# Between two MLPs: the second sequence's rows, sums and operands placed anew around the first quads

## The chip, the cores and the metric

The kernel runs on one NeuronCore of a Trainium2 chip. The metric is the device time of one execution in microseconds; lower is better.

## What is computed

Three layers follow each other: a block-wise linear attention with decay, an MLP with a squared relu, and a gated MLP with a norm in front. Cut to what matters here:

```python
x = attn_out.transpose(0, 2, 1, 3).reshape(B * S, H * D)    # 2 sequences x 768 tokens, 512 features

h = x @ w_in                                  # first MLP, 512 -> 2048
x = (s * relu(h) ** 2 + b) @ w_out            # 2048 -> 512

rms = np.sqrt(np.mean(x * x, axis=-1, keepdims=True) + 1e-06)
xn = x / rms * rms_g                          # the norm between the MLPs
g = xn @ w_gate                               # second MLP, 512 -> 1536
val = xn @ w_val
return (silu(g) * val) @ w_out
```

All of it is float32. A float32 product is made of three matmuls in a reduced format (`PASSES`): each operand is split into a high part (a copy that rounds) and a low part (what is left), and high x high, high x low and low x high are summed in PSUM.

## The kernel before

Tokens lie along the free dimension and features along the 128 partitions. A sequence is 768 tokens; a product over one takes 512 and 256 columns.

**First MLP.** `for blk in range(B)` goes over the two sequences, and within a block `it` goes over 16 tiles of hidden features. TensorE makes the hidden tile of `it` (`h` and `hb`, one bank each) and adds the products of the tile before to `y` (four banks, 512 tokens each) and `z` (two banks, two pieces of 256 tokens in each). ScalarE and VectorE make relu, square, scale and the split of the tile (`relu2`, `gate_hi1`, `gate_lo1`; the split goes to the tile `g`). Beside that, prepared work is drawn from a list `todo`: `work(n)` runs the next n tasks at a fixed place of an iteration.

**Between the MLPs.** When a block's sums are done, `take` and `take2` bring them from PSUM to the rows `xq[blk]`, times the norm's gain `g_col`; `square` writes their squares to `xtmp[blk]`. `norm_total` adds the squares of the four feature tiles on VectorE; `norm_rstd` sums over partitions on TensorE (`nps`), takes the power -1/2 on GpSimd and lays it on a diagonal (`affine_select`); `norm_apply` broadcasts it by a matmul with ones (`rb`) and scales the rows on VectorE. `x_tasks` then makes the seven operands of the second MLP from the rows: four differences t1 to t4 (`sub`) and seven splits (`x_split`: ScalarE writes the high part, VectorE the low part). For the first sequence all this lies inside the second block. For the second it lies in the first quads.

**Second MLP.** Gate, value, the two halves of the features and the two halves of a sequence's tokens form 2 x 2 blocks, multiplied with seven block products in place of eight. A *quad* (`quad(i)`) is one tile of 128 hidden features on one sequence: seven products of six matmuls of 384 columns, in four PSUM banks, quads 0, 2, 4 in banks 0 to 3 and quads 1, 3, 5 in banks 4 to 7. Products b0, b1, b2, b3 come first; ScalarE copies b0 (`q1`), and VectorE's adds `add(u2, b1, q1)`, `add(u3, b2, u2)`, `add(u3, b3, u3)` carry the sums on. Then three products are added on top in b0, b2 and b3 (called b0', b2', b3' below); b2' may start when the add from b2 is done, b3' when the add from b3 is. ScalarE makes the two silus, and `a_mult` multiplies silu and value, one quad later. Quads 0 to 3 take the first sequence, quad 4 is the first on the second; from quad 8 on both alternate.

**What sets the order.** The schedule is manual: every engine runs its instructions as the code emits them, in order. A quad yields after parts of its products; at each `(quad, part)` the table `plan` says which tasks of the second sequence are emitted, and `work()` draws from `todo` (weight tasks). Weight set f of the second MLP is made by `w_tasks(f)`, six tasks with scalings, four GpSimd sums and splits; sets 0 to 3 in the second block, but for the last three tasks of set 3 (`w_last`), which stand in `plan`. Before, parts 0, 1 and 2 of a quad end after the add from b1, after the add from b3, and at its end.

**Rooms.** `xq0` and `xq1` hold the rows, `g` the first MLP's split tile. Squares of the second sequence go to `g` (`xtmp.append(rows(m_g))`), operands of the second sequence lie in `xs`, `xq0` and `wm`, and later products of `a_mult` in `g`.

VectorE's take and ScalarE's square of one PSUM bank are ordered one behind the other by a wait, in the order of the code.

Of the kernel before, what the change touches and what calls it, by code (L numbers as in the profile page):

```python
# [22 lines left out]
def attention_moe_moe2_kernel(  # L23
# [40 lines left out]
    NG1 = 4  # L64
# [469 lines left out]
    xtmp = [xq[1]]  # L534
# [11 lines left out]
    def x_tasks(s, other):  # L546
        b11, b12, b21, b22 = (x_block(s, k, h) for k in range(2) for h in range(2))
        t1, t2, t3, t4 = (x_sum(s, i) for i in range(4))

        def sub(engine, to, a, b):  # L550
            engine.tensor_tensor(to, a, b, op=ALU.subtract)

        def first():
            sub(nc.vector, t1, b12, b11)
            sub(nc.vector, t2, b22, t1)

        def second():
            sub(other, t3, b22, b12)
            sub(other, t4, b21, t2)
            x_split(s, B11, b11)  # L560

        rest = ((T2, t2), (T3, t3), (T1, t1), (B21, b21), (T4, t4), (B22, b22))
        return [first, second] + [lambda op=op, src=src: x_split(s, op, src) for op, src in rest]
# [4 lines left out]
    def norm_total(s):  # L568
        x = xtmp[s]
        nc.vector.tensor_tensor(x[:, 0:2], x[:, 0:2], x[:, 2:4], op=ALU.add)  # L570
        nc.vector.tensor_tensor(x[:, 0], x[:, 0], x[:, 1], op=ALU.add)

# [19 lines left out]
    def norm_apply(s, cols, ps):  # L592
        nc.tensor.matmul(ps, ones, xtmp[s][:, 1, cols], start=True, stop=True)
        width = cols.stop - cols.start
# [18 lines left out]
    for blk in range(B):  # L613
# [4 lines left out]
        for it in range(NF1 + 1):  # L618
# [39 lines left out]
            work(blk)  # L658
# [11 lines left out]
            work(2 * blk)  # L670
            if blk == 0 and it == NF1 - 1:
                split_x(xs1, xq[1])
            if blk == 1:
                if it == 0:
                    norm_total(0)
                if it == 2:
                    norm_rstd(0, other)
                if it in (3, 4, 5):
                    norm_apply(0, slice((it - 3) * BX, (it - 2) * BX), other)
                if it == 5:  # L680
                    todo += x_tasks(0, nc.vector)
                    load_w(0, 0)
                    load_w(0, 1)
                if it == 8:
                    words = piece(early, "u1", 8, F32)
                    tasks = [w_tasks(f) for f in range(NG1)]
                    todo += sum(tasks, [])[:-3]
                    w_last = tasks[-1][-3:]

        if blk == 1:  # L690
            m_g = piece(early, "g", 12, F32)
            xtmp.append(rows(m_g))
# [20 lines left out]
        for d in (0, 2):  # L713
            square(NK + d // 2)
            take2(d)
            take2(d + 1)
# [4 lines left out]
    m_x2, m_wm2 = piece(early, "xq0", 12), piece(early, "wm", 6)  # L721
# [272 lines left out]
```

## Time and profile before

| | |
|---|---|
| median of 3 runs | 614.87 us (613.70 to 615.73) |
| profiled execution | 612.44 us, of which the span on the core is 610.6 us |
| TensorE matmul busy | 597.2 us, 98% of the span |
| TensorE weight loads | 540.3 us, 88% |
| VectorE, ScalarE, GpSimd busy | 368.8 us (60%), 299.1 us (49%), 72.5 us (12%) |
| chain that ended last | TensorE 90%, VectorE 5%, ScalarE 2% |

The profile gives one execution, in microseconds from the span's start. PE is TensorE, DVE VectorE, ACT ScalarE, POOL GpSimd. A row of a timeline is one instruction or several of one kind that follow each other; in square brackets stands how long the engine was idle before it and what released it. Rows of a timeline can overlap by some 0.1 us, since an engine starts an instruction before the last is quite done. The first block ends near 184 us, the second near 322 us, the quads run from there to about 507 us, and the output product ends the kernel.

### The profile page before, as it was taken

To read this page: it belongs to the slowest core of one execution; us is meant where nothing else is said; L and a number is where in the kernel's file an instruction comes from. 1 tells how busy PE (TensorE), PEld (TensorE's weight loads), DVE (VectorE), ACT (ScalarE), POOL (GpSimd) and SP (SyncE) were. 2 spreads that over 40 slices of the span, in tenths; PEclk is the share of its full clock that TensorE was granted. 3 is DMA by queue.
4 is the path that set the end of the run, shared out by engine and by line. 5 is a ranking of instruction groups with operands and counts; after the bars stand their busy time and mean duration, and the time that the engine had idled before them with its cause. 6 is when DMAs were issued, how large, how long until landed. Compare 5 with 4: busy or idle time off the path is not lost.

```text
span 610.6 us, 9226 instructions
## 1 busy us (share of the span) xinstructions
PE 597.2 (98%) x3654; PEld 540.3 (88%) x3654; DVE 368.8 (60%) x610; ACT 299.1 (49%) x549; POOL 72.5 (12%) x80
## 2 busy tenths in 40 slices
PE   8999999999999999999998799999999999999997
PEld 7888888888888888888887799999999998888886
DVE  6786776666745135444445976777777777875200
ACT  5685665565556224555554233444444445764200
POOL 3550000000000100011101500222222200000000
PEclk8999999999999999999999989999999999999999
DMA  8992533333100000022220001222122122220300
GB/s 321 368 347 96 181 116 127 130 112 138 69 1 1 0 2 1 0 70 70 69 69 2 0 2 39 90 79 70 69 70 70 69 70 70 104 104 0 139 34 35
DMA packets 17281, 51.97 MB, mean 85 GB/s; under 512 B 2390, under 2 KB 2390, under 8 KB 17238
## 3 DMA queue, kind: packets, MB, share of 16 engines
q1 hardware_dynamic: 17232, 51.39, 23.6%
q8 instruction: 28, 0.46, 0.3%
q14 instruction: 15, 0.12, 0.1%
q10 hardware_dynamic: 6, 0.00, 0.0%
HBM read 48.24 MB, written 3.15 MB: 84 GB/s over the span
## 4 chain that ended last, share of the span: by engine, by line
PE 90%; DVE 5%; ACT 2%; issue 1%; DMA 1%; SPq 0%; DVEq 0%; ACTq 0%
PE q L744 25%; PE out L886 16%; PE h L228 14%; PE y L631 14%; PE hb L228 7%; PE z L641 7%; PE sc L328 2%; PE o L370 2%; PE o L379 2%; PE st L396 1%; DMA k<-in_kT_dram 1%; DVE xs_None L150 1%; DVE r_None L755 1%; DVE xq_None L598 1%; DVE xq_None L702 1%
## 5 line engine op out<-in xcount | busy, mean ns | idle before, releaser
L744 PE MATMUL q<-u_None,u_None 128*128 128x384 f32 x504 | 91.9, 340 | 5.0 <-DVE st_None L755 3.6
L228 PE MATMUL h<-xs_None,u_None 128*128 128x512 f32 x384 | 94.1, 394 | 0.5 <-ACT r_None L241 0.5
L744 PEld LDWEIGHTS q<-u_None,u_None 128*128 128x128 f32 x504 | 88.9, 191 | 6.1 <-DVE st_None L755 4.2
L631 PE MATMUL y<-g_None,u_None 128*128 128x512 f32 x384 | 93.2, 391 | 0.0
L228 PEld LDWEIGHTS h<-xs_None,u_None 128*128 128x128 f32 x384 | 70.2, 188 | 14.3 <-ACT r_None L241 0.7
L631 PEld LDWEIGHTS y<-g_None,u_None 128*128 128x128 f32 x384 | 70.1, 188 | 13.3
L247 DVE TENSOR_SCALAR r_None<-r_None,params 128x768 f32<-128x768 f32 x32 | 21.8, 682 | 87.4 <-ACT r_None L243 87.4
L744 PE MATMUL q<-xs_None,u_None 128*128 128x384 f32 x288 | 55.2, 334 | 0.0
L641 PEld LDWEIGHTS z<-g_None,u_None 128*128 128x128 f32 x384 | 50.3, 191 | 2.5
L228 PEld LDWEIGHTS hb<-xs_None,u_None 128*128 128x128 f32 x384 | 50.3, 191 | 2.5
L641 PE MATMUL z<-g_None,u_None 128*128 128x256 f32 x384 | 51.0, 282 | 0.0
L228 PE MATMUL hb<-xs_None,u_None 128*128 128x256 f32 x384 | 51.0, 282 | 0.0
L241 ACT ACTIVATE r_None<-h 128x512 f32<-128x512 f32 x32 | 19.1, 598 | 64.1 <-PE h L228 63.0
L744 PEld LDWEIGHTS q<-xs_None,u_None 128*128 128x128 f32 x288 | 50.4, 188 | 0.0
L147 ACT ACTIVATE u_None<-u_None 128x768 fp32r<-128x768 f32 (+3 forms) x39 | 31.6, 822 | 32.7 <-DVE u_None L144 28.2
L253 DVE TENSOR_TENSOR g_None<-r_None,g_None 128x768 fp32r<-128x768 f32 x32 | 30.7, 958 | 24.6 <-ACT g_None L249 24.6
L150 DVE TENSOR_TENSOR u_None<-u_None,u_None 128x512 fp32r<-128x512 f32 (+2 forms) x51 | 37.6, 769 | 3.6 <-ACT u_None L147 3.5
L791 ACT ACTIVATE st_None<-r_None 128x384 f32<-128x384 f32 x24 | 12.6, 525 | 52.6 <-DVE r_None L755 52.6
L755 DVE TENSOR_TENSOR st_None<-q,r_None 128x384 f32<-128x384 f32 x48 | 26.5, 552 | 19.1 <-PE q L744 19.0
L512 POOL TENSOR_TENSOR u_None<-u_None 128x256 f32<-128x256 f32 x12 | 14.9, 1240 | 177.1 <-DVE u_None L144 177.1
L147 ACT ACTIVATE u_None<-wm_None 128x512 fp32r<-128x512 f32 x32 | 20.0, 625 | 27.9 <-DVE wm_None L144 27.9
L886 PE MATMUL out<-u_None,xs_None 128*128 128x512 f32 x144 | 32.8, 389 | 0.0
(138 smaller groups left out, 905.4 us busy)
## 6 DMA issues: line engine op xcount, KB each, us to landing
st_None<-in_w_dram SPq DMA_DIRECT2D x68, 512.0 KB, 3.3
kv<-in_kv_dram SPq DMA_DIRECT2D x12, 512.0 KB, 6.0
q<-in_qT_dram SPq DMA_DIRECT2D x12, 256.0 KB, 5.8
k<-in_kT_dram SPq DMA_DIRECT2D x12, 256.0 KB, 5.8
out_dram<-st_None SPq DMA_DIRECT2D x8, 256.0 KB, 2.5
out_dram<-u_None SPq DMA_DIRECT2D x4, 256.0 KB, 3.9
row<-in_lam_dram ACTq DMA_DIRECT2D x1, 0.0 KB
row<-in_s_dram ACTq DMA_DIRECT2D x1, 0.0 KB
```

The lines of the kernel that those rows point to most:

```text
L147: nc.scalar.activation(to, src, AF.Copy)
L150: nc.vector.tensor_tensor(to, src, hi.bitcast(F32), op=ALU.subtract)
L228: nc.tensor.matmul(ps, wt[:, wi, kk * P : (kk + 1) * P], xs[:, xi, kk, cols], start=n == 0, stop=n == 3 * NK - 1)
L241: nc.scalar.activation(r[:, 0:BT], ps[0], AF.Relu)
L247: nc.vector.tensor_scalar(r, r, s_col, b_col, op0=ALU.mult, op1=ALU.add)
L253: nc.vector.tensor_tensor(g2[:, 1, :], r, g2[:, 0, :].bitcast(F32), op=ALU.subtract)
L512: nc.gpsimd.tensor_tensor(s1, a21, a22, op=ALU.add)
L631: nc.tensor.matmul(acc[d], wt[:, wi, d * P : (d + 1) * P], gs[f][:, gi, 0:BT], start=f == 0 and pi == 0, stop=f == NF1 - 1 and pi == 2,)
L641: nc.tensor.matmul(acc2[d // 2][:, d % 2 * BX : (d % 2 + 1) * BX], wt[:, wi, d * P : (d + 1) * P], gs[f][:, gi, BT:BW], start=f == 0 and p ...
L744: nc.tensor.matmul(ps, w_set(f)[:, wi, wop * KC + kt * P : wop * KC + (kt + 1) * P], x_ops[s][xop][:, xi, kt, :], start=n == 0 and not mor ...
L755: nc.vector.tensor_tensor(to, ps, more, op=ALU.add)
L886: nc.tensor.matmul(ps, rows_[:, ai], w_out[f][:, wi, :], start=first and pi == 0, stop=last and pi == 2)
```

## The change

- The second sequence's squares go to `xq0` instead of `g`. Its operands four and five lie in `g` instead of `xq0`, and what lay in `g` later (a room of `a_mult`, three output weights) changes places with it likewise.
- `take2`, the 256-token takes, run on VectorE instead of ScalarE, in both blocks. In the second block, the second square of z and all four `take2` are emitted in quad 0 instead of ahead of it.
- A quad yields five times instead of three: after the copy of b0, after the add from b1, after the add from b2, after the add from b3, and at its end. `work()` runs at the three places where it ran.
- `norm_total` is two steps with the third add of quad 0 between them, and the sums over partitions follow the first product of quad 1 instead of all of quad 0. The broadcasts go to banks 2 and 3, and the two halves of the scaling are emitted at two places.
- `x_tasks` is eleven steps of one instruction or one split each, all differences on VectorE. For the second sequence two of the differences were on GpSimd. They stand at eleven places of quads 2 to 4, where eight tasks stood in quads 1 to 4.
- `a_mult` of quads 1, 2 and 3 runs on GpSimd instead of VectorE.
- In the second block, `work` draws by a table: the eleven tasks of the first sequence in iterations 6 and 7, all 24 weight tasks in iterations 8 to 15. Before, it drew three an iteration and left the last three weight tasks to the quads.

```diff
-    xtmp = [xq[1]]
+    xtmp = [xq[1], xq[0]]
...
-    def x_tasks(s, other):
+    def x_tasks(s):
+
         b11, b12, b21, b22 = (x_block(s, k, h) for k in range(2) for h in range(2))
         t1, t2, t3, t4 = (x_sum(s, i) for i in range(4))
...
+        return [
+            sub(t1, b12, b11),
+            sub(t2, b22, t1),
+            split(B11, b11),
+            split(T2, t2),
+            sub(t3, b22, b12),
+            split(T3, t3),
+            split(T1, t1),
+            split(B21, b21),
+            sub(t4, b21, t2),
+            split(T4, t4),
+            split(B22, b22),
+        ]
...
-            work(blk)
+            if blk:
+                work()
...
-            work(2 * blk)
+            if blk:
+                work({6: 4, 7: 5, 9: 1, 10: 3, 11: 2, 12: 3, 13: 3, 14: 2, 15: 2}.get(it, 0))
...
-            nc.scalar.activation(xq[blk][:, d, BT:BW], ps, AF.Copy, scale=g_col[:, d : d + 1])
+            nc.vector.tensor_scalar(xq[blk][:, d, BT:BW], ps, g_col[:, d : d + 1], None, op0=ALU.mult)
...
-        for d in (0, 2):
-            square(NK + d // 2)
-            take2(d)
-            take2(d + 1)
+        square(NK)
+        if blk == 0:
+            square(NK + 1)
+            for d in range(NK):
+                take2(d)
...
-            nc.vector.tensor_tensor(a_at[order[q]], v_both, silu, op=ALU.mult)
+            (nc.gpsimd if 1 <= q < NG1 else nc.vector).tensor_tensor(a_at[order[q]], v_both, silu, op=ALU.mult)
...
-        (0, 1): [lambda: norm_total(1)],
-        (0, 2): [lambda: start_second(0), w_last[0]],
-        (1, 0): [w_last[1]],
-        (1, 1): [lambda: start_second(1)],
-        (1, 2): [xt[0]],
-        (2, 0): [w_last[2], xt[1]],
-        (2, 1): [xt[2]],
-        (2, 2): [xt[3]],
-        (3, 0): [xt[4]],
-        (3, 1): [xt[5]],
-        (3, 2): [xt[6]],
-        (4, 0): [xt[7]],
-        (23, 0): [lambda: split_first(0)],
+        (0, 0): [lambda: square(NK + 1), lambda: take2(0), lambda: take2(1)],
+        (0, 2): [lambda: next(total)],
+        (0, 3): [lambda: next(total)],
+        (0, 4): [lambda: take2(2), lambda: take2(3)],
+        (1, 0): [lambda: norm_rstd(1, bank(1, "nps1"))],
+        (1, 3): [spread],
+        (1, 4): [lambda: scale[1]()],
+        (2, 0): xt[0:1],
+        (2, 1): xt[1:2],
+        (2, 3): xt[2:3],
+        (2, 4): xt[3:4],
+        (3, 0): xt[4:5],
+        (3, 1): xt[5:6],
+        (3, 2): xt[6:7],
+        (3, 4): xt[7:8],
+        (4, 0): xt[8:9],
+        (4, 1): xt[9:10],
+        (4, 2): xt[10:11],
+        (23, 1): [lambda: split_first(0)],
```

**ScalarE, from the end of the second block to quad 0's copy.** `y` and `z` are the block's sums, `q_0` is bank b0 of quad 0; the brackets name what a row waits for. Before:

```order
L696 ACTIVATE g_None<-y_1_1903 128x512 [waits DVE_49,PE_49]
L696 ACTIVATE g_None<-y_0_1902 128x512 [waits DVE_49]
L696 ACTIVATE g_None<-y_3_1905 128x512
L696 ACTIVATE g_None<-y_2_1904 128x512 [waits DVE_49]
L699 ACTIVATE g_None<-z_0_1906 128x2x256
L706 ACTIVATE xq_5_None<-z_0_1906,g_col 128x256 x2
L699 ACTIVATE g_None<-z_1_1907 128x2x256
L706 ACTIVATE xq_5_None<-z_1_1907,g_col 128x256 x2
L771 ACTIVATE st_20_None<-q_0_2916 128x384 [waits PE_49]
```

After:

```order
L704 ACTIVATE xq_4_None<-y_1_1903 128x512 [waits PE_49]
L704 ACTIVATE xq_4_None<-y_0_1902 128x512 [waits DVE_49]
L704 ACTIVATE xq_4_None<-y_3_1905 128x512 [waits PE_49]
L704 ACTIVATE xq_4_None<-y_2_1904 128x512 [waits DVE_49]
L707 ACTIVATE xq_4_None<-z_0_1906 128x2x256 [waits PE_49]
L780 ACTIVATE st_18_None<-q_0_2919 128x384 [waits PE_49]
L707 ACTIVATE xq_4_None<-z_1_1907 128x2x256
```

The four takes (L706) have left the engine, the squares go to another tile, and the copy of b0 has moved up by five instructions.

**VectorE, quad 3.** L755, then L764, are a quad's adds from PSUM (`q_1` to `q_3` are its banks b1 to b3), L763 is `a_mult`, L150 the low part of a split, L551, then L552, a difference. Before, from the add from b1 to that from b3':

```order
L755 TENSOR_TENSOR r_None<-q_1_3124,st_20_None 128x384
L150 TENSOR_TENSOR xs_None<-g_None,xs_None 128x768
L755 TENSOR_TENSOR st_20_None<-q_2_3125,r_None 128x384
L755 TENSOR_TENSOR st_20_None<-q_3_3126,st_20_None 128x384
L150 TENSOR_TENSOR xs_None<-xq_5_None,xs_None 128x768
L755 TENSOR_TENSOR st_20_None<-q_2_3125,r_None 128x384
L755 TENSOR_TENSOR r_None<-q_3_3126,r_None 128x384
```

After:

```order
L150 TENSOR_TENSOR g_None<-xq_4_None,g_None 128x768
L552 TENSOR_TENSOR xq_4_None<-xq_5_None 128x768
L764 TENSOR_TENSOR r_None<-q_1_3118,st_18_None 128x384
L150 TENSOR_TENSOR g_None<-xq_4_None,g_None 128x768
L764 TENSOR_TENSOR st_18_None<-q_2_3119,r_None 128x384
L150 TENSOR_TENSOR xs_None<-xq_4_None,xs_None 128x768
L764 TENSOR_TENSOR st_18_None<-q_3_3120,st_18_None 128x384
L764 TENSOR_TENSOR st_18_None<-q_2_3119,r_None 128x384
L764 TENSOR_TENSOR r_None<-q_3_3120,r_None 128x384
```

Each add from b1, b2 and b3 now has one piece of the second sequence ahead of it, and `a_mult` is no longer among the rows.

**GpSimd, quads 0 to 4.** L580, then L588, is the power, L582, then L590, the diagonal, L512 to L515 are sums of a weight set. Before:

```order
L580 TENSOR_TENSOR rstd_2981<-ms_2979,neg_half 128x6
L582 AFFINE_SELECT g_None<-rstd_2981 128x768
L512 TENSOR_TENSOR u_16_None<-u_16_None 128x256
L513 TENSOR_TENSOR u_16_None<-u_16_None 128x256
L514 TENSOR_TENSOR u_16_None<-u_16_None 128x256
L515 TENSOR_TENSOR u_16_None<-u_16_None 128x256
L551 TENSOR_TENSOR g_None<-xq_5_None 128x768
L551 TENSOR_TENSOR g_None<-xq_5_None,g_None 128x768
```

After:

```order
L514 TENSOR_TENSOR u_16_None<-u_16_None 128x256
L515 TENSOR_TENSOR u_16_None<-u_16_None 128x256
L588 TENSOR_TENSOR rstd_3000<-ms_2998,neg_half 128x6
L590 AFFINE_SELECT xq_4_None<-rstd_3000 128x768
L772 TENSOR_TENSOR u_19_None<-st_18_None 128x768 x3
```

The sums of weight set 3 have gone ahead of the power, into the block, and three multiplies stand where two differences stood.

## Rows read from the trace of the kernel before

**Rows 1.** Timeline of TensorE: start, duration, line, operation, out<-in, count; undisturbed quads.

```profile
375.26 1.20 PE L744 MATMUL q<-wm_None,u_None 128*128 128x384 f32 x6
...
382.54 1.20 PE L744 MATMUL q<-wm_None,u_None 128*128 128x384 f32 x6
```

**Rows 2.** Timeline of TensorE, quads 0 to 4, idle before in brackets.

```profile
321.69 4.33 PE L744 MATMUL q<-u_None,u_None 128*128 128x384 f32 x24
327.43 3.61 PE L744 MATMUL q<-u_None,u_None 128*128 128x384 f32 x18 [1.41 <-ACT st_None L771]
332.00 1.50 PE L576 MATMUL nps<-ones,g_None 128*128 128x1 f32 x12 [0.96 <-DVE g_None L571]
...
337.61 1.45 PE L593 MATMUL rb<-g_None,ones 128*128 128x384 f32 x4
338.60 8.79 PE L744 MATMUL q<-u_None,u_None 128*128 128x384 f32 x48
350.96 11.24 PE L744 MATMUL q<-u_None,u_None 128*128 128x384 f32 x54 [3.57 <-DVE st_None L755]
...
367.86 1.31 PE L744 MATMUL q<-wm_None,u_None 128*128 128x384 f32 x6 [0.46 <-DVE st_None L755]
369.02 2.24 PE L744 MATMUL q<-xs_None,u_None 128*128 128x384 f32 x12
```

**Rows 3.** Windows: from:to, length, busy PE, PEld, DVE, ACT, POOL, granted clock, DMA share, GB/s.

```profile
352.00:354.00 2.00, 2.00 (x9) 2.00 (x8) 0.94 (x3) 0.00 (x0) 0.00 (x0) 0.63 0.00 0
354.00:356.00 2.00, 2.00 (x8) 2.00 (x8) 0.62 (x2) 1.32 (x3) 0.00 (x0) 0.52 0.00 0
```

**Rows 4.** Timeline of ScalarE: first squares, quad 0's copy, and a high part.

```profile
321.89 1.58 ACT L696 ACTIVATE g_None<-y 128x512 f32<-128x512 f32 x3 [4.20 <-PE z L641]
...
326.84 0.54 ACT L771 ACTIVATE st_None<-q 128x384 f32<-128x384 f32 x1
...
355.04 0.82 ACT L147 ACTIVATE xq_None<-g_None 128x768 fp32r<-128x768 f32 x1
```

**Rows 5.** Timeline of VectorE: a take, the scalings, a difference, a multiply, two adds.

```profile
318.88 0.74 DVE L702 TENSOR_SCALAR xq_None<-y,g_col 128x512 f32<-128x512 f32 x1
...
338.45 3.54 DVE L598 TENSOR_TENSOR xq_None<-xq_None,rb 128x768 f32<-128x768 f32 x4
...
343.04 1.76 DVE L551 TENSOR_TENSOR g_None<-xq_None 128x768 f32<-128x768 f32 x1
...
345.79 0.95 DVE L763 TENSOR_TENSOR u_None<-st_None 128x768 f32<-128x768 f32 x1
346.66 0.55 DVE L755 TENSOR_TENSOR r_None<-q,st_None 128x384 f32<-128x384 f32 x1
...
369.21 0.56 DVE L755 TENSOR_TENSOR st_None<-q,r_None 128x384 f32<-128x384 f32 x1 [0.74 <-PE q L744]
```

**Rows 6.** Timeline of GpSimd: the power and the two differences.

```profile
333.78 1.72 POOL L580 TENSOR_TENSOR rstd<-ms,neg_half 128x6 f32<-128x6 f32 x1 [27.78 <-DVE ms L578]
335.56 0.86 POOL L582 TENSOR_SCALAR_AFFINE_SELECT g_None<-rstd 128x768 f32<-128x768 f32 x1
...
342.14 1.85 POOL L551 TENSOR_TENSOR g_None<-xq_None 128x768 f32<-128x768 f32 x1 [2.11 <-DVE xq_None L598]
345.95 2.47 POOL L551 TENSOR_TENSOR g_None<-xq_None,g_None 128x768 f32<-128x768 f32 x1 [1.96 <-DVE g_None L551]
```

**Rows 7.** Timeline of ScalarE and TensorE at the end of block 0.

```profile
187.83 0.87 ACT L706 ACTIVATE xq_None<-z,g_col 128x256 f32<-128x256 f32 x2
...
189.24 3.02 PE L228 MATMUL h<-xs_None,u_None 128*128 128x512 f32 x12 [0.53 <-ACT r_None L241]
...
197.71 2.91 PE L228 MATMUL h<-xs_None,u_None 128*128 128x512 f32 x12
```

**Rows 8.** Timeline of TensorE near the start, and the window behind it.

```profile
7.91 2.08 PE L328 MATMUL sc<-q,k 64*128 64x128 f32 x16 [1.59 <-DMA k<-in_kT_dram]
...
8.40:11.80 3.40, 3.40 (x46) 3.18 (x45) 3.37 (x10) 2.31 (x10) 0.71 (x1) 0.59 1.04 404
```

More of the change, by code (lines that the diff above doesn't have):

```diff
@@ L544, in x_split, with sub, split @@
         split_lo(x_ops[s][op][:, 1], src, x_ops[s][op][:, 0])
-    def x_tasks(s, other):
+    def x_tasks(s):
         b11, b12, b21, b22 = (x_block(s, k, h) for k in range(2) for h in range(2))
         t1, t2, t3, t4 = (x_sum(s, i) for i in range(4))
[L550 to L563, printed above, removed]
+        def sub(to, a, b):
+            return lambda: nc.vector.tensor_tensor(to, a, b, op=ALU.subtract)
+        def split(op, src):
+            return lambda: x_split(s, op, src)
+        return [
[11 more added lines that the diff above has]
+        ]
     NTT = BW // P
@@ L678, in attention_moe_moe2_kernel @@
                 if it in (3, 4, 5):
-                    norm_apply(0, slice((it - 3) * BX, (it - 2) * BX), other)
+                    norm_apply(0, slice((it - 3) * BX, (it - 2) * BX), other)()
                 if it == 5:
-                    todo += x_tasks(0, nc.vector)
+                    todo += x_tasks(0)
                     load_w(0, 0)
                     load_w(0, 1)
-                if it == 8:
+                if it == 7:
                     words = piece(early, "u1", 8, F32)
[L686 to L692, printed above, removed]
+                    for f in range(NG1):
+                        todo += w_tasks(f)
         def square(d):
@@ L712, in attention_moe_moe2_kernel @@
             square(d)
-        for d in (0, 2):
-            square(NK + d // 2)
-            take2(d)
-            take2(d + 1)
+        square(NK)
[3 more added lines that the diff above has]
+                take2(d)
     order = [(f, s) for s in range(B) for f in range(NG1)] + [(f, s) for f in range(NG1, NF2) for s in range(B)]
-    m_x2, m_wm2 = piece(early, "xq0", 12), piece(early, "wm", 6)
-    x_ops.append([x_place(m_x, i) for i in range(4)] + [x_place(m_x2, 0), x_place(m_x2, 1), x_place(m_wm2, 0)])
+    m_wm2 = piece(early, "wm", 6)
+    x_ops.append([x_place(m_x, i) for i in range(4)] + [x_place(m_g, 0), x_place(m_g, 1), x_place(m_wm2, 0)])
     m_tmp = piece(early, "st1", 8, F32)
@@ L817, in attention_moe_moe2_kernel @@
     last_room = {}
-    w_out = [hi_lo(at(m_u[3], 4 * i, 4)) for i in range(7)] + [hi_lo(at(m_x2, 4 * i, 4)) for i in range(3)]
+    w_out = [hi_lo(at(m_u[3], 4 * i, 4)) for i in range(7)] + [hi_lo(at(m_g, 4 * i, 4)) for i in range(3)]
     w_out.append(hi_lo(at(m_wm2, 0, 4)))
@@ L873, in attention_moe_moe2_kernel @@
             f = (i + 3) // 2
-            if part == 1 and i % 2 and NG1 <= f < NF2:
+            if part == 3 and i % 2 and NG1 <= f < NF2:
                 todo += w_tasks(f)
-            if (i, part) == (21, 1):
+            if (i, part) == (21, 3):
                 load_out(0)
@@ L879, in attention_moe_moe2_kernel @@
                 todo += out_tasks(0) + out_tasks(1)
-            work()
+            if part in (1, 3, 4):
+                work()
     a_mult()
```

24 lines of the change are left out of this document (15 added, 9 removed).

## Prediction

> **What bounds the kernel now.** TensorE sets the end: outside one stretch its matmuls follow each other without a gap. I read the timeline of TensorE first, from the end of the first MLP's second block (321.7 us). A quad, the second MLP's unit, is 42 matmuls and takes 7.28 us when nothing holds it (382.54 less 375.26, the same product of two quads [rows 1]): 0.173 a matmul, 1.04 a product of six. Quad 0 starts at 321.69. Quad 4, the first on the second sequence, ends with the product after the one at 369.02, so at 370.06 [rows 2]. That is 48.37 us for five quads, the sums for the norm (1.4, its 1.50 less the overlap with what follows) and two broadcasts (0.99, 337.61 to 338.60). Without a wait it would be 36.4 + 2.4 = 38.8, so **9.6 us are lost there**: gaps of 1.41, 0.96, 3.57 and 0.46 us [rows 2], some 1.7 at half clock behind the long one (granted 0.63 and 0.52 over four microseconds [rows 3]), the rest in small pieces.
>
> Next I asked which wait ends last before each gap. The first two begin at ScalarE: the squares of the block's output start only at 321.89, when the last matmul of the block is done, 4.20 us after ScalarE went idle [rows 4], since they are written over the tile g that those matmuls read. Ten ScalarE instructions, six squares and four takes, stand from there to quad 0's copy at 326.84. The 3.57 us gap ends when VectorE has done an add of quad 2 (TensorE goes on at 350.96): ahead of it on VectorE stood four scalings, two differences and pieces of the last weight set, some of them held up by GpSimd [rows 5, 6].
>
> **A lock that the rows show.** VectorE's difference at 343.04 reads two SBUF operands and took 1.76 us, against 0.95 for the two-SBUF multiply at 345.79; GpSimd ran from 342.14 to 343.99 [rows 5, 6]. GpSimd's next, begun at 345.95 under that VectorE multiply, took 2.47 instead of 1.85. The add from PSUM at 346.66 took 0.55 under the same GpSimd instruction: unharmed. So GpSimd's work and VectorE's two-SBUF work exclude each other, and the walk below is made so.
> The Trainium skill, SBUF — State Buffer, section "Who interferes with whom", says the same of VectorE with two SBUF inputs against a GpSimd instruction that reads SBUF: whichever starts first has the shared ports and the other blocks. It speaks against this change, which puts three multiplies on GpSimd beside VectorE's splits (2.7 us of the walk's end, as rival D works out).
>
> **Squares and takes.** The squares now go to xq0, which nothing in the block still reads, and only the last waits for the last matmul. VectorE first finishes weight set 3: its low parts wait for the block's last but one products, which end half an iteration (4.2 of 8.4 us [rows 7]) ahead of 321.7, at 317.5; so its first take starts near 319.7 instead of 318.88 [rows 5]. Takes and squares alternate per bank at 0.7 each at the most (0.74 the row): fourth square at 322.4, z's first square 322.9, quad 0's copy 323.4 instead of 327.4. The four 256-wide takes move from ScalarE (0.87 for two [rows 7]) to VectorE. No row shows one there; it lies between nothing, if VectorE idles, and the 0.56 of a 384-wide add [rows 5]; I take 0.4. Quad 0's third product needs its bank at 323.8 and finds it free: the gap of 1.41 goes. The sum of squares (twice a 768-wide piece) now stands between quad 0's second and third add; by then TensorE is two products ahead, and quad 0 ends near 329.0. Its norm sums come behind quad 1's first product, so the 0.96 goes too.
>
> **Quads 1 to 4, walked row by row** along the new order, with 0.47 to 0.56 an add, 0.87 a scaling or two-SBUF piece of 768 [rows 5], 0.82 a ScalarE copy of 768 and 0.54 one of 384, a silu alike [rows 4], 1.72 + 0.86 GpSimd's power and diagonal [rows 6], and a product readable 0.19 after its last issue (the next one's start at 369.02, the add's at 369.21 [rows 2, 5]):
> - Quad 1: norm sums done 331.4, diagonal 334.5, just when the broadcasts come up. Ends 338.6, no gap.
> - Quad 2: scaling done 341.0; the first difference must wait for GpSimd's multiply of quad 1 (340.0 to 341.8); its second add (b2) ends 344.5 where TensorE wants it at 343.9: gap 0.7. Ends 346.6.
> - Quad 3: the split of T2 is ready at 348.7, GpSimd's second multiply holds the ports to 349.8; then come the third difference, an add and T3 before the b2 add, at 353.9 instead of 351.9: gap 2.1, and 0.3 behind it. Ends 356.3.
> - Quad 4: the split of B21 ready at 358.4, third multiply to 359.5; then fourth difference, add, T4, add: 363.6 instead of 361.5. Gap 2.1 and 0.3. Ends 366.0.
>
> So five quads end at 366.0 where they ended at 370.06: **4.1 us** gained. Afterwards TensorE is ahead again and everything shifts by that.
>
> **Block 0's end.** ScalarE's two pairs of z takes stand before the relu of the next block, and TensorE waited 0.53 us for it [rows 7]. They go to VectorE, which then has time until the next block's first g is wanted: **0.5 us** gained; between 0 and 0.53.
>
> **The rest at nothing.** Eleven x tasks of the first sequence stand in two iterations instead of eight in three, and the three tasks of weight set 3 move back into the block. An iteration is 8.4 us (189.24 to 197.71 [rows 7]); walked alike, the gate of iteration 7 is done 2.7 us before its products, and the relu of iteration 8 2.2 us before its bank is wanted. If that cover is gone, each is a gap of its excess. SP's queue has the same order. xq0 and g change places as rooms; each is free when first written.
>
> **The clock.** A gap can cost a second time. Behind 3.57 us of idle the granted clock fell to the lower of its levels (1.2 instead of 2.4 GHz) and cost 1.7 us; at the start a gap of 1.59, among small matmuls, was followed by 0.59 over 3.4 us [rows 8]; the gaps of 1.41 and 0.96 were followed by none. The new gaps of 2.1 stand between. I charge one such stretch in quads 3 and 4 together, **1.5 us** (VectorE's lag hides some of it), with bounds 0 and 3.
> The Trainium skill, TensorE: Matmul & The Clock Gate, section "HAM oscillation", puts the fall down to idle gaps longer than those that I expect; by that rule it wouldn't come, which is rival B below. The start of this trace speaks against it.
>
> **Sum.** The profiled execution takes 612.44 (span 610.6 and 1.84 around it). 612.44 - 4.1 - 0.5 + 1.5 = 609.3. It lies 2.43 under the median of the three runs, so the median becomes 614.87 - 3.1 = **611.8**.
>
> **The rivals** (a difference of under 0.3%, 1.84 us, can't be told from none here):
> - B, no fall of the clock: 610.3. For it: the gaps of the walk are split by a product or so, and 1.41 was harmless. 0.28.
> - C, a fall in both quads: 613.4, no measurable change. For it: both gaps are alike. 0.14.
> - D, the lock does not hold, or the multiplies find VectorE on adds only: the same walk without it loses 0.1 in quad 2 and 1.3 each in quads 3 and 4, and ends 2.7 earlier at 363.3; no fall: 612.44 - 6.8 - 0.5 + 2.43 = 607.6. Against it: three rows. 0.06.
> - E, the change doesn't do what it says: squares or norm wait on something else, and the gaps come back at other adds. Under 1 of the 4.6 is left: 614 to 615. Against it: the new order names no such wait. 0.06.
> - F, slower: the exclusion works both ways in every quad. If each multiply costs VectorE its whole 1.85 instead of the 0.7 to 1.1 above (it starts just as a split does), the gaps of quads 2 to 4 grow by 2.6 in all to some 3 each and every one brings a clock fall: 4.6 - 2.6 - 3 x 1.7 = -3.1, so 618.0. It decides where a gap comes near the 3.57 us that did this before. 0.05.
>
> **Chances.** Forecast 0.41. Faster are the forecast, B and D, 0.75; within 0.3% C and E, 0.20; slower F, 0.05. The range 609.0 to 613.8 holds the forecast, B and C with half a microsecond around them, 0.83.
>
> **What would show it.** Squares starting near 319 and quad 0's copy near 323.4; no gap in quads 0 and 1; the b2 adds of quads 2, 3 and 4 late by about 0.7, 2.1 and 2.1; three GpSimd multiplies of 1.85 and VectorE pieces of 1.6 to 2 beside them; one stretch of low clock. Wrong would be gaps in iterations 6 to 15 of the second block, or a gap at quad 0's takes.

## The result and the profile after

The changed kernel takes 609.45 us (median of 5 runs, 609.36 to 612.21), the kernel before 614.94 (5 runs, 613.70 to 616.45): a ratio of 0.992 (95% interval 0.989 to 0.994). The profiled execution is 609.45 with a span of 607.6; before it was 612.44 and 610.6. The engines' busy times (us, share of the span, instructions) hardly differ from those before:

```profile
PE 596.3 (98%) x3654; PEld 539.2 (89%) x3654; DVE 372.8 (61%) x617; ACT 296.6 (49%) x541; POOL 74.9 (12%) x81
```

The forecast was 611.8, inside its range but 2.3 us too slow. Faster was the right sign, and most of the mechanism came as told. But the measured time lies only 0.45 us above the lower end of the range: the sum has wrong terms that cancel by luck in the profiled execution, and one more that shows in the median.

The timeline of TensorE after, over quads 0 to 4 (start, duration, line, operation, out<-in, count, idle time before and its releaser; L753 is the quads' line, L584 the norm's sums, L601 the broadcasts). It answers to [rows 2]:

```profile
321.60 8.49 PE L753 MATMUL q<-u_None,u_None 128*128 128x384 f32 x48
329.92 1.39 PE L584 MATMUL nps<-ones,xq_None 128*128 128x1 f32 x12
331.18 3.37 PE L753 MATMUL q<-u_None,u_None 128*128 128x384 f32 x18
334.57 1.56 PE L601 MATMUL rb<-xq_None,ones 128*128 128x384 f32 x4
335.67 8.79 PE L753 MATMUL q<-u_None,u_None 128*128 128x384 f32 x48
345.07 7.58 PE L753 MATMUL q<-u_None,u_None 128*128 128x384 f32 x42 [0.61 <-DVE st_None L764]
354.65 2.65 PE L753 MATMUL q<-u_None,u_None 128*128 128x384 f32 x12 [2.00 <-DVE st_None L764]
...
364.60 1.31 PE L753 MATMUL q<-wm_None,u_None 128*128 128x384 f32 x6 [2.08 <-DVE st_None L764]
365.93 2.32 PE L753 MATMUL q<-xs_None,u_None 128*128 128x384 f32 x12
368.09 2.24 PE L753 MATMUL q<-g_None,u_None 128*128 128x384 f32 x12
```

The gaps of 1.41, 0.96 and 3.57 us are gone, and three stand in their place: 0.61, 2.00 and 2.08, all behind an add on VectorE. Quad 5 starts 1.04 (a product) ahead of the last row, at 367.05. So quads 0 to 4 take 45.45 us, where they took 48.37 [rows 2].

Ahead of the quads, the first product of the first MLP, before and then after, and the product after that had the wait of 0.53 at the end of block 0 [rows 7]:

```profile
48.40 3.03 PE L228 MATMUL h<-xs_None,u_None 128*128 128x512 f32 x12
```

```profile
49.15 3.06 PE L228 MATMUL h<-xs_None,u_None 128*128 128x512 f32 x12
...
189.34 2.91 PE L228 MATMUL h<-xs_None,u_None 128*128 128x512 f32 x12
```

From that first product to quad 0 the kernel before takes 273.29 us and the changed one 272.45. The 0.84 gained there hardly shows in quad 0's start (321.69, then 321.60), because the first MLP began 0.75 later in this execution. Behind quad 4 nothing differs: from the start of quad 5 to the end of the span it is 240.5 to 240.6 us in every profiled execution of this document.

The other engines in the same stretch, ScalarE, VectorE and GpSimd in turn (L704 squares, L780 the copy of b0, L714 the 256-token takes, L552 a difference, L150 the low part of a split, L764 adds, L772 the multiplies). They answer to [rows 4 to 6]:

```profile
319.00 0.60 ACT L704 ACTIVATE xq_None<-y 128x512 f32<-128x512 f32 x1 [1.75 <-PE y L642]
...
322.84 0.49 ACT L780 ACTIVATE st_None<-q 128x384 f32<-128x384 f32 x1
```

```profile
322.79 0.88 DVE L714 TENSOR_SCALAR xq_None<-z,g_col 128x256 f32<-128x256 f32 x2 [0.49 <-ACT xq_None L707]
...
341.49 1.72 DVE L552 TENSOR_TENSOR xq_None<-xq_None 128x768 f32<-128x768 f32 x1
...
349.43 1.97 DVE L150 TENSOR_TENSOR g_None<-xq_None,g_None 128x768 fp32r<-128x768 f32 x1 [1.39 <-ACT g_None L147]
...
354.05 0.55 DVE L764 TENSOR_TENSOR st_None<-q,r_None 128x384 f32<-128x384 f32 x1
...
359.28 1.97 DVE L150 TENSOR_TENSOR xs_None<-xq_None,xs_None 128x768 fp32r<-128x768 f32 x1 [1.39 <-ACT xs_None L147]
```

```profile
340.55 1.85 POOL L772 TENSOR_TENSOR u_None<-st_None 128x768 f32<-128x768 f32 x1 [6.03 <-ACT st_None L802]
348.74 1.85 POOL L772 TENSOR_TENSOR u_None<-st_None 128x768 f32<-128x768 f32 x1 [6.34 <-ACT st_None L802]
358.59 1.85 POOL L772 TENSOR_TENSOR u_None<-st_None 128x768 f32<-128x768 f32 x1 [8.01 <-ACT st_None L802]
```

The squares start at 319.00 and the copy at 322.84 (319 and 323.4 were foretold). Each GpSimd multiply has a VectorE piece under it that takes 1.72, 1.97 and 1.97 us where such a piece takes 0.95 alone [rows 5]; TensorE goes on when the add at 354.05 is done, two pieces and two adds behind the held split.

The granted clock behind the second and third gap (windows: from:to, length, busy PE, PEld, DVE, ACT, POOL, granted clock, DMA share, GB/s), which answers to [rows 3]:

```profile
356.00:358.00 2.00, 2.00 (x11) 2.00 (x12) 1.11 (x2) 0.01 (x1) 0.00 (x0) 1.00 0.00 0
...
366.00:368.00 2.00, 2.00 (x12) 2.00 (x13) 1.06 (x2) 0.10 (x1) 0.00 (x0) 1.00 0.00 0
```

In this execution the clock stayed at its upper level (1.00) there.

### The profile page after: what moved, and what is told of

Its sections match the earlier page's. It is cut to its first block, busy times and chain, and to the rows that moved or that the text cites. A ratio compares the mean times of both kernels' runs of the same rounds, so it can differ in the third digit from the quotient of the medians.

```text
span 607.6 us, 9225 instructions
## 1 busy us (share of the span) xinstructions
PE 596.3 (98%) x3654; PEld 539.2 (89%) x3654; DVE 372.8 (61%) x617; ACT 296.6 (49%) x541; POOL 74.9 (12%) x81
## 4 chain that ended last, share of the span: by engine, by line
PE 95%; DVE 2%; issue 1%; DMA 1%; ACT 1%; SPq 0%; ACTq 0%; DVEq 0%
PE q L753 26%; PE out L906 16%; PE h L228 15%; PE y L642 14%; PE hb L228 8%; PE z L652 8%; PE o L370 2%; PE sc L328 2%; PE o L379 2%; PE st L396 1%; DMA k<-in_kT_dram 1%; DVE r_None L764 0%; DVE st_None L764 0%; DVE xq_None L552 0%; ACT g_None L147 0%
## 5 line engine op out<-in xcount | busy, mean ns | idle before, releaser
L753 PE MATMUL q<-u_None,u_None 128*128 128x384 f32 x504 | 90.4, 336 | 2.6 <-DVE st_None L764 2.6
L753 PEld LDWEIGHTS q<-u_None,u_None 128*128 128x128 f32 x504 | 87.3, 188 | 3.9 <-DVE st_None L764 3.6
L753 PE MATMUL q<-xs_None,u_None 128*128 128x384 f32 x288 | 55.3, 334 | 0.0
L753 PEld LDWEIGHTS q<-xs_None,u_None 128*128 128x128 f32 x288 | 50.3, 188 | 0.3 <-issue 0.3
L150 DVE TENSOR_TENSOR u_None<-u_None,u_None 128x512 fp32r<-128x512 f32 (+2 forms) x51 | 37.6, 768 | 7.3 <-ACT u_None L147 7.0
L764 DVE TENSOR_TENSOR st_None<-q,r_None 128x384 f32<-128x384 f32 x48 | 26.5, 552 | 20.1 <-PE q L753 20.0
L512 POOL TENSOR_TENSOR u_None<-u_None 128x256 f32<-128x256 f32 x12 | 14.2, 1184 | 150.9 <-DVE u_None L144 99.0
```

Source lines behind the costliest of these rows:

```text
L150: nc.vector.tensor_tensor(to, src, hi.bitcast(F32), op=ALU.subtract)
L512: nc.gpsimd.tensor_tensor(s1, a21, a22, op=ALU.add)
L753: nc.tensor.matmul(ps, w_set(f)[:, wi, wop * KC + kt * P : wop * KC + (kt + 1) * P], x_ops[s][xop][:, xi, kt, :], start=n == 0 and not mor ...
L764: nc.vector.tensor_tensor(to, ps, more, op=ALU.add)
```

## The experiments

Twelve runs were made: seven edited kernels, and five repeats of the changed kernel or the kernel before. e1 to e4 shared a chip, so did e5 to e8, and so did e9 to e12; ratios are to the kernel before on the same chip (612.92 us on the first, median of 19; 614.76 on the second, median of 28). Besides the time, one number is used for all of them: from the start of quad 0 to the start of quad 5, as 45.45 above. A stretch is a time in which TensorE runs at the lower of its two clock levels (1.2 instead of 2.4 GHz, granted 0.50).

### Which part of the change brings what

**e1_rooms_alone** gives the kernel before the new place for its squares, with the exchange of rooms that goes with it, and nothing else (cut):

```diff
-    xtmp = [xq[1]]
+    xtmp = [xq[1], xq[0]]
...
-            m_g = piece(early, "g", 12, F32)
-            xtmp.append(rows(m_g))
```

> The kernel before, with one part of the change alone: the second sequence's squares go to xq0 instead of g, and the rooms of xq0 and g change places. Theory (the squares waited for the last matmuls that read g): the squares start near 319 instead of 321.9, quad 0's copy comes near 324.7 instead of 327.4, the gaps of 1.41 and 0.96 us shrink to under 0.3 together, the long gap in quad 2 stays, since VectorE's row of work before it is only moved as a whole: about 2.0 us less than before, ratio 0.997. Rival (what gained was the unloading of the quads, the room did nothing): ratio 1.000.

Measured: 610.51 us, ratio 0.996 (0.993 to 0.998), 2.4 less than before. TensorE in quads 0 to 4:

```profile
320.84 7.45 PE L740 MATMUL q<-u_None,u_None 128*128 128x384 f32 x42
328.48 1.50 PE L576 MATMUL nps<-ones,xq_None 128*128 128x1 f32 x12 [0.18 <-DVE xq_None L571]
...
347.47 11.24 PE L740 MATMUL q<-u_None,u_None 128*128 128x384 f32 x54 [3.57 <-DVE st_None L751]
```

Quad 0 runs without a gap and the norm's gap has shrunk from 0.96 to 0.18; 3.57 and the low clock behind it stay, and so does the 0.54 at the end of block 0. Quads 0 to 4 take 45.75, against 48.37 of before with the same low clock: 2.6 us. So **in the profiled executions the room of the squares alone brings nearly all that the whole change brings in the quads** (2.9). All the rest there exchanges one gap of 3.57 for 0.61, 2.00 and 2.08, and where the clock falls behind one of these too, it is even a little behind (46.30 in e5, below). In the medians the room alone brings 2.4, the whole change 5.1 (e5). The rest goes with the end of block 0 (0.8, e8) and with the clock: the middle one of e1's runs has a mean granted clock of 0.994, that of the changed kernel in e5 0.997, some 1.8 us of full speed.

**e2_mult_twice** issues each of the three GpSimd multiplies twice; **e3_mult_on_vector** puts them back on VectorE:

```diff
-            (nc.gpsimd if 1 <= q < NG1 else nc.vector).tensor_tensor(a_at[order[q]], v_both, silu, op=ALU.mult)
+            for _ in range(2 if 1 <= q < NG1 else 1):
+                (nc.gpsimd if 1 <= q < NG1 else nc.vector).tensor_tensor(a_at[order[q]], v_both, silu, op=ALU.mult)
```

```diff
-            (nc.gpsimd if 1 <= q < NG1 else nc.vector).tensor_tensor(a_at[order[q]], v_both, silu, op=ALU.mult)
+            nc.vector.tensor_tensor(a_at[order[q]], v_both, silu, op=ALU.mult)
```

> The changed kernel, with GpSimd's multiplies of quads 1, 2 and 3 each issued twice, to the same place. Theory (GpSimd's multiply keeps VectorE's two-SBUF work waiting): the first difference, the low part of T2 and that of B21 each wait 1.85 us longer; the gaps of 0.61, 2.00 and 2.08 us in quads 2, 3 and 4 become 2.5, 3.9 and 3.9: 5.5 us more, 615, and up to 5 more where the clock falls behind them. Rival (the gaps come from the length of the chain silu, split, difference, copy, split, add, the multiply lies beside it): within 0.5 us of the changed kernel's 609.45.

> The changed kernel, with all of a_mult on VectorE as before the change. Theory (the port lock costs about 1 us in quads 3 and 4, and 0.8 in quad 2): the two low parts take 0.95 instead of 1.97 us, the difference 0.95 instead of 1.72, and 0.87 of multiply comes into VectorE's row each time; by the walk the gaps become 0.6, 1.35 and 1.4: 1.3 us less than the changed kernel, 608.1. Rival (moving the multiplies to GpSimd was a gain): gaps grow by 0.87 each, 612.

Measured: twice 617.03, ratio 1.006 (1.003 to 1.008); on VectorE 607.12, ratio 0.989 (0.984 to 0.993). The gaps of TensorE, first with the multiplies twice, then on VectorE:

```profile
345.36 7.56 PE L753 MATMUL q<-u_None,u_None 128*128 128x384 f32 x42 [1.79 <-DVE st_None L764]
356.56 3.40 PE L753 MATMUL q<-u_None,u_None 128*128 128x384 f32 x12 [3.64 <-DVE st_None L764]
...
368.91 2.26 PE L753 MATMUL q<-wm_None,u_None 128*128 128x384 f32 x6 [2.93 <-DVE st_None L764]
```

```profile
344.18 7.56 PE L753 MATMUL q<-u_None,u_None 128*128 128x384 f32 x42 [0.71 <-DVE st_None L764]
353.07 2.65 PE L753 MATMUL q<-u_None,u_None 128*128 128x384 f32 x12 [1.33 <-DVE st_None L764]
...
362.34 1.30 PE L753 MATMUL q<-wm_None,u_None 128*128 128x384 f32 x6 [1.42 <-DVE st_None L764]
```

On VectorE the gaps of quads 3 and 4 are 0.7 shorter each, although VectorE now does the multiply (0.95) as well; the splits there take 0.96 again. Twice, they grow to 3.64 and 2.93 (3.9 each was expected, and 2.5 in quad 2 where 1.79 came), and the clock falls at both (granted 0.54 from 358 to 360 and from 370 to 372). How the two engines take turns, GpSimd first, then VectorE, with the multiplies twice:

```profile
349.01 4.35 POOL L773 TENSOR_TENSOR u_None<-st_None 128x768 f32<-128x768 f32 x2 [4.98 <-ACT st_None L803]
```

```profile
349.70 1.97 DVE L150 TENSOR_TENSOR g_None<-xq_None,g_None 128x768 fp32r<-128x768 f32 x1 [1.39 <-ACT g_None L147]
351.59 2.58 DVE L552 TENSOR_TENSOR xq_None<-xq_None 128x768 f32<-128x768 f32 x1
```

Two multiplies need 4.35, not 3.7: the second stood 0.65 while VectorE did its split, and the difference behind that then took 2.58. So each instruction has the ports for itself, and the engines alternate. That is also why the gaps came out shorter than expected. The lock is shown, from both sides; rival D is out, and the three multiplies on GpSimd are a part of the change that costs: 45.45 against 44.20 with them on VectorE, 1.25 us, neither with a stretch at the lower clock in the quads.

**e4_splits_earlier** emits four of the eleven steps a part earlier, so that no split begins just behind a multiply; **e6_adds_first** besides puts the first two differences one part later:

```diff
-        (2, 3): xt[2:3],
-        (2, 4): xt[3:4],
-        (3, 0): xt[4:5],
+        (2, 3): xt[2:4],
+        (2, 4): xt[4:5],
...
-        (3, 4): xt[7:8],
-        (4, 0): xt[8:9],
+        (3, 3): xt[7:8],
+        (3, 4): xt[8:9],
```

```diff
-        (2, 0): xt[0:1],
-        (2, 1): xt[1:2],
+        (2, 1): xt[0:1],
+        (2, 2): xt[1:2],
```

> The changed kernel, with the splits of T2 and B21 emitted one place earlier (behind the add from b3, ahead of the end of the quad), and the third and fourth difference at the end of the quad, ahead of GpSimd's multiply. Theory (the gaps of quads 3 and 4 are the low parts of T2 and B21, which come only behind the silu and then wait for GpSimd): by the walk the b2 add of quad 3 comes at 352.3, that of quad 4 at 359.5, where TensorE wants them at 352.35 and 359.9; gaps of 0.6 in quad 2 as before, 0.3 and 0 in quads 3 and 4: about 4.5 us less, 605. Rival (VectorE as such has too much to do in quads 3 and 4, wherever the pieces stand): the gaps move to other adds, less than 1 us gained.

> The kernel of e4 (splits of T2 and B21 one place earlier), and in quad 2 the first difference behind the add from b1 instead of ahead of it, the second behind the add from b2. Theory (every gap left is an add that stands behind one two-SBUF piece too many): the gap of 0.62 in quad 2 goes, no gap over 0.2 us between quad 0 and the end of quad 4, 5.3 us less than the changed kernel, 0.6 less than e4. Rival (quad 2's gap is GpSimd's multiply, whatever stands ahead of the add): the gap stays or moves to the add from b3.

Measured: 605.76, ratio 0.986 (0.982 to 0.991), and 604.84, ratio 0.984 (0.980 to 0.987). TensorE with the first, then with both:

```profile
345.83 10.05 PE L753 MATMUL q<-u_None,u_None 128*128 128x384 f32 x54 [0.62 <-DVE st_None L764]
```

```profile
336.39 18.80 PE L753 MATMUL q<-u_None,u_None 128*128 128x384 f32 x102
```

The first keeps only the gap of quad 2, the second lists none: quads 0 to 4 take 40.68 and 40.02, where the prediction's count without any wait is 38.8. GpSimd still has the multiplies, and with both edits VectorE's pieces beside them take 1.26, 1.61 and 1.33. The **version with both is faster than either kernel**, by 4.8 us than the changed one on the same chip.

**e7_set3_back** gives the last three tasks of weight set 3 back to the quads; **e8_takes_on_scalar** gives the 256-token takes back to ScalarE, in both blocks:

```diff
-        (0, 4): [lambda: take2(2), lambda: take2(3)],
+        (0, 4): [lambda: take2(2), lambda: take2(3), w_last[0]],
...
+        (1, 1): [w_last[1]],
...
-        (2, 1): xt[1:2],
+        (2, 1): [w_last[2], xt[1]],
```

```diff
-            nc.vector.tensor_scalar(xq[blk][:, d, BT:BW], ps, g_col[:, d : d + 1], None, op0=ALU.mult)
+            nc.scalar.activation(xq[blk][:, d, BT:BW], ps, AF.Copy, scale=g_col[:, d : d + 1])
```

> The changed kernel with one part undone: the last three tasks of weight set 3 stand in quads 0 to 2 again (at the end of quad 0, behind the add from b1 of quad 1, behind that of quad 2). Theory (VectorE and GpSimd must have as little as can be before the second sequence's operands are done): GpSimd's four sums (about 3 us) stand ahead of the power, the broadcasts wait some 1.7 us for the diagonal, and VectorE has 2.7 us more, of which quad 2 shows some 2: 3 to 4.5 us more than the changed kernel, and more where the clock falls. Rival (the weight tasks lie beside other work there): under 1 us.

> The changed kernel with one part undone: the 256-token takes on ScalarE again, in both blocks. Theory: at the end of block 0 TensorE waits again 0.5 us for the relu behind the four takes; in quad 0 the copy of b0 comes 0.75 later, at 324.1, where it is not wanted before 325.9: 0.5 us more than the changed kernel in all, less than these rounds tell. Rival (the takes on ScalarE held quad 0 as well): 1.5 us or more.

Measured: 614.81, ratio 1.001 (0.998 to 1.003), the whole gain gone; and 611.22, ratio 0.995 (0.993 to 0.997). GpSimd and TensorE with the tasks back in the quads:

```profile
331.01 0.74 POOL L513 TENSOR_TENSOR u_None<-u_None 128x256 f32<-128x256 f32 x1 [19.44 <-DVE u_None L144]
331.71 1.46 POOL L514 TENSOR_TENSOR u_None<-u_None 128x256 f32<-128x256 f32 x1
333.13 1.44 POOL L515 TENSOR_TENSOR u_None<-u_None 128x256 f32<-128x256 f32 x1
334.54 1.33 POOL L588 TENSOR_TENSOR rstd<-ms,neg_half 128x6 f32<-128x6 f32 x1
```

```profile
336.86 2.93 PE L601 MATMUL rb<-xq_None,ones 128*128 128x384 f32 x4 [2.46 <-POOL xq_None L590]
...
350.03 7.58 PE L754 MATMUL q<-u_None,u_None 128*128 128x384 f32 x42 [1.81 <-DVE st_None L765]
```

Three sums of the weight set stand on GpSimd ahead of the norm's power (L588), which starts at 334.54 instead of 331.60; the broadcasts wait 2.46 for its diagonal, quad 2's add is late by 1.81, the clock falls twice in the quads (granted 0.53 from 338 to 340, 0.56 from 362 to 364), and quads 0 to 4 take 51.60. Three tasks that the prediction filed under "the rest at nothing" are worth 5.1 us of the median (3 to 4.5 and more with the clock were expected), once the norm has been drawn forward: that move is what lets it keep its place.

With the takes on ScalarE the wait at the end of block 0 is back, the same as in [rows 7]:

```profile
188.97 3.02 PE L228 MATMUL h<-xs_None,u_None 128*128 128x512 f32 x12 [0.54 <-ACT r_None L241]
```

TensorE comes to quad 0 0.67 later than in e5's execution, though 0.13 earlier at the last products of block 0 (184.10 against 184.23): 0.8 us for that end. Quad 0 shows no new gap, and quads 0 to 4 take 45.72, so the rival (the takes held quad 0 as well) is not borne out, though the median is 1.5 above e5's. Its profiled execution took 609.33 at a mean clock of 0.999, while the middle one of its runs has 0.994 and that of e5's 0.997. So the rest goes with stretches at the lower clock that its profile does not hold, and why there are more of them stays open.

### Where the median stands above the profiled execution

**e5_after_again** is the changed kernel on the second chip; **e9**, **e10** and **e11** are the kernel before, **e12** the changed one, unchanged, for other executions.

> The changed kernel unaltered, on the same chip as the three beside it, to have them compared with it and not only with the kernel before. Expected: gaps of 0.6, 2.0 and 2.1 us in quads 2, 3 and 4 as in its first profile, ratio to the kernel before 0.991 to 0.993. Where an execution is slower by 2 to 3 us, the granted clock of the core stands at 0.992 instead of 0.996 (a stretch of low clock behind the gaps).

> The kernel before, unchanged, profiled once more: where do its executions that take some 615 us spend the 2.4 us by which they lie above the profiled 612.44? Theory H1, stretches at the lower clock: the profiled execution had two, at a mean granted clock of 0.994; the runs of before at 0.992 have spans of 612.1 to 614.0, those at 0.989 have 614.6 to 615.0. If this execution shows a mean clock of 0.992 and a span of 612 to 614, it has a third stretch at the lower clock, behind a gap that stayed at full clock before (1.41 or 0.96 in quads 0 and 1, or 0.53 at the end of block 0). Theory H2, something else: the span is 612 to 614 with two stretches, and the wait for the first chunks of k at the start or another gap is longer by about 2 us. If the span is near 610.6 again with 0.994, nothing is learned of the two.

> The kernel before once more, for another execution. H1, stretches at the lower clock: the span goes with the count of such stretches, two at a mean clock of 0.994 and 610.6 to 612, three at 0.992 and 612 to 614, four at 0.989 and about 615. H2, something else: spans that differ by 2 us at equal counts, by the wait at the start or another gap.

> The kernel before a third time, for another execution. H1, stretches at the lower clock: as many as the mean clock tells (two at 0.994, three at 0.992, four at 0.989), each about 1.5 us of span. H2, something else: spans that differ by 2 us at equal counts.

> The changed kernel, unchanged, for another execution. H1, stretches at the lower clock: a span of about 606.2 with none (mean clock 0.999), 607.6 with one (0.997, at the start or behind the 2.0 us gap of quad 3), 610.7 to 611.3 with three (0.990 to 0.992, at the start and behind both gaps of 2 us). H2, something else: a span of 611 with one stretch and a longer wait elsewhere.

Measured: e5 609.67 us (11 runs, 608.16 to 613.11), ratio 0.993 (0.990 to 0.996); e9 616.71, e10 612.08, e11 614.95, e12 608.91, one execution each. Where each of them, and the two first profiles, ran at the lower clock:

| execution | span, us | mean clock | stretches at the lower clock | quads 0 to 4, us |
|---|---|---|---|---|
| before, profiled | 610.6 | 0.994 | start; behind 3.57 | 48.37 |
| before, e10 | 610.4 | 0.996 | start | 47.53 |
| before, e11 | 613.2 | 0.992 | behind 0.96; behind 3.57, twice as long | 51.12 |
| before, e9 | 614.9 | 0.989 | start, twice as long; behind 0.94; behind 3.57 | 50.02 |
| after, profiled | 607.6 | 0.996 | start | 45.45 |
| after, e5 | 607.5 | 0.997 | behind 2.01 (quad 3) | 46.30 |
| after, e12 | 606.4 | 0.999 | none | 45.50 |

The windows behind the gaps, e10 behind 3.57, then e11 behind 0.96 and behind 3.57, then e5 and e12 behind 2.01 (columns as above):

```profile
352.00:354.00 2.00, 2.00 (x14) 2.00 (x13) 1.55 (x4) 0.00 (x0) 0.00 (x0) 1.00 0.00 0
354.00:356.00 2.00, 2.00 (x13) 2.00 (x12) 0.61 (x2) 1.39 (x3) 0.00 (x0) 1.00 0.00 0
```

```profile
334.00:336.00 2.00, 2.00 (x10) 2.00 (x9) 1.06 (x2) 1.22 (x2) 1.93 (x2) 0.64 0.00 0
...
352.00:354.00 2.00, 1.56 (x5) 1.56 (x6) 1.81 (x3) 0.00 (x0) 0.00 (x0) 0.50 0.00 0
354.00:356.00 2.00, 2.00 (x8) 2.00 (x7) 0.56 (x1) 0.00 (x0) 0.00 (x0) 0.50 0.00 0
356.00:358.00 2.00, 2.00 (x8) 2.00 (x7) 0.56 (x1) 0.66 (x2) 0.00 (x0) 0.50 0.00 0
```

```profile
354.00:356.00 2.00, 1.98 (x9) 1.66 (x9) 1.59 (x3) 0.00 (x0) 0.00 (x0) 0.84 0.04 8
356.00:358.00 2.00, 2.00 (x8) 2.00 (x8) 0.56 (x1) 0.13 (x1) 0.00 (x0) 0.50 0.00 0
358.00:360.00 2.00, 2.00 (x11) 2.00 (x10) 0.83 (x1) 1.59 (x3) 1.53 (x1) 0.81 0.00 0
```

```profile
356.00:358.00 2.00, 2.00 (x13) 2.00 (x12) 0.56 (x1) 1.22 (x3) 0.61 (x1) 1.00 0.00 0
```

The gaps are the same in every execution of a kernel (1.41, 0.94 to 0.96 and 3.57 before; 0.62, 2.01 and 2.09 after, when nothing slows TensorE). What differs is whether the clock falls behind them: behind 3.57 in three executions of four, behind 0.94 to 0.96 in two of four, behind 2.0 in one of three. "Behind" says where the stretch begins; that this gap alone brings it is not shown. In e11 the stretch in quad 1 begins 2.7 us after the 0.96 has ended, and between them lie the norm's sums, matmuls of one column.

For before the time of the quads follows the count of stretches in them, the one twice as long counted twice: 47.53, 48.37, 50.02 and 51.12 for none, one, two and three. So **H1 holds** there. The stages ahead of the first MLP differ too, and not with the wait for k alone: that wait was 1.07 in e11 and 2.71 in e12, whose first product of the first MLP starts at 48.27 and 47.96. In e9, with the longest wait (3.03) and the low clock at the start twice as long, it starts at 51.02. So 2.6 of the 4.3 us by which e9's span is above the profiled one lie ahead of the first MLP, and how they split between wait and clock stays open: there H2 has a part. The profiled execution of before had 0.994; 14 of its 28 runs on the second chip have 0.992 or 0.993, with spans of 612.1 to 614.0, and four have less. By its mean clock a median execution of before thus has a stretch more than the profiled one, and its span lies 1.5 to 3.4 above: the size of the 2.43 by which the median of the first three runs lay above it.

## Why the prediction was right, and where it was not

**The squares and takes: right.** First square at 319.00, copy at 322.84, no gap in quads 0 and 1, the 256-token take 0.44 (0.4 was taken). e1 isolates the squares.

**The end of block 0: right in kind, a little small.** The 0.53 [rows 7] is gone, and e8 brings it back with the takes. From the first MLP to quad 0 the gain is 0.84 where 0.5 was charged: the bracket holds only the listed idle time.

**The lock: right.** Gaps of 0.7, 2.1 and 2.1 were foretold; 0.61, 2.00 and 2.08 came, at the adds that were named. The Trainium skill, SBUF — State Buffer, section "Who interferes with whom", speaks of an exclusive lock and of issue order deciding who blocks; the 1.97 for 0.95 agrees, and e2 and e3 show that the rule speaks against this part of the change, as the prediction said, by 1.25 us.

**The quads' gain of 4.1: too large by 1.2.** It came to 2.9 (48.37 less 45.45). The failing step is the walk's end at 366.0 for five quads, 44.3 us, where 45.45 was measured. Quad 1 ended at 339.09 instead of 338.6, quad 2 at 347.28 instead of 346.6, quad 3 at 357.14 instead of 356.3, quad 4 at 367.05 instead of 366.0: 0.5, then 0.2 us more in each. Most of the 0.5 lies at the broadcasts, priced at 0.99. They take 1.10 (334.57 to 335.67), and the row of 48 matmuls behind them takes 8.79, where the row of 48 in quad 0 takes 8.49: 0.3 more, all of it between its first matmul and its second. The 8.79 stood already in [rows 2]. In the later quads the listed gaps came out 0.1 shorter than told, but 0.3, 0.6 and 0.6 us stand in no bracket, where the walk had 0, 0.3 and 0.3. Without low clock on either side the gain is 2.0 (47.53 of e10 less 45.50 of e12).

**The clock's charge of 1.5: wrong in the profiled execution, and wrongly sized.** No stretch followed the gaps of 2.00 and 2.08, which is rival B's mechanism, and its 610.3 lay nearer to the measured time than the forecast. In e5 one did, behind the same gap. Its price there is 0.8 us (46.30 less 45.45 or 45.50), since TensorE, slowed, then waits only 1.30 instead of 2.08 in quad 4:

```profile
353.76 3.43 PE L753 MATMUL q<-u_None,u_None 128*128 128x384 f32 x12 [2.01 <-DVE st_None L764]
...
364.49 1.28 PE L753 MATMUL q<-wm_None,u_None 128*128 128x384 f32 x6 [1.30 <-DVE st_None L764]
```

The prediction had named this cover ("VectorE's lag hides some of it") and still charged nearly the whole 1.7. Before, the stretch behind 3.57 cost no more (48.37 less 47.53 of e10). Where the next gap does not get shorter, the price is larger: behind the 0.96 in e11 the next 24 matmuls took 6.00, against 4.41 in e10, and the gap after them was 3.57 in both.

**The offset of 2.43: the step that made the miss.** The sum came to 609.3 for the profiled execution and 609.45 was measured. That is luck: the quads' gain was put 1.2 too high, the clock's charge 1.5 too high, block 0's end 0.3 too low, and the first MLP began 0.75 later in this execution than in the profiled one of before, for no reason that the change gives (47.96 to 51.02 over the executions of both kernels in the table). Then the distance from before's profile to its median was carried over as if it were a fixed addition. It is not: by the mean clocks it is mostly low-clock stretches that before's median execution has and its profiled one has not, and the changed kernel's profiled execution already is a median one (0.996 to 0.997, four of five runs). Charging the new gaps for the clock and keeping an offset that is made of the old gaps' clock counted it twice. This is worked out from e9 to e11 and the mean clocks of 28 runs; the three runs of which the 2.43 was taken have no clock on record but the profiled one's.

**What the change brings, then.** Over all runs on the second chip the means are 614.62 (28) and 610.35 (11): 4.3 us. The two idle terms are 2.0 in the quads and 0.8 at block 0's end, which leaves 1.5. The time missing to full clock, the span times one less the mean clock, averaged over the same runs, is 4.6 before and 2.8 after; its 1.8 covers the rest, with a little over, as a stretch can hide in a wait or in the last microseconds, when TensorE is done. So some third of the gain is clock. That split is worked out from averages and was not isolated by a run.

**"The rest at nothing": one item was not.** Nothing was lost in the block, as told (TensorE lists no gap in the second block). But the move of weight set 3's last tasks, costed at nothing, carries the gain of the quads (e7).

**Rival F** was the nearest alarm: in e2, with the multiplies' time doubled, the gaps of quads 3 and 4 and two falls of the clock came as it described, and the time was slower than before by 0.6%.

## What to carry to other kernels

Before a sum is moved from a profiled execution to the median, look at the mean granted clock of each run: where the profiled one differs from the median one, the difference is part of the kernel's own gaps and changes with them. Work moved to GpSimd is not free for VectorE when both read SBUF: put it where VectorE reads PSUM, or move VectorE's pieces a slot (4.8 us for six steps of a table here). And in a walk along an order, set the measured row of a run of matmuls beside an undisturbed row of the same count (8.79 against 8.49 here), since waits too small to be listed are in it.

## What the runs showed of the hardware

- The same gap is or is not followed by a fall of TensorE's clock, by execution: 3.57 us without one in e10, 2.01 us with and without (e5, e12), 0.94 us with one (e9). The Trainium skill, TensorE: Matmul & The Clock Gate, section "HAM oscillation", ties the fall to a single idle gap longer than any of 0.94 to 2.1; the fall behind 2.01 in e5 and the missing one behind 3.57 in e10 differ from it, and here the measurement decides. The falls in e9 and e11 differ too as far as the 0.94 to 0.96 is their cause, which is not shown.
- A stretch at the lower level cost 0.8 us of time in e5 (and 1.6 behind the 0.96 in e11, where the next gap was 3.57 as in e10), though the granted clock over its six microseconds (0.84, 0.50, 0.81) takes 1.7 us of full speed from TensorE: in e5 the next wait for VectorE is shorter by 0.8.
- With two GpSimd multiplies in a row, VectorE's waiting two-SBUF instruction came in between: the pair took 4.35 us instead of 3.7, and VectorE's two pieces 1.97 and 2.58 instead of 0.95 each. An add from PSUM beside them kept its 0.55.
- The wait for the first chunks of k differed from 1.07 to 3.03 us between executions of the kernel before, and the start of its first MLP from 48.27 to 51.02.
